# The beginning of a delta-rule attention and MoE kernel, put in one written list of steps: blocks turned by corner products, both first q loads early

## The chip, the cores and the metric

The kernel runs on one core of one Trainium2 chip. The metric is the time of one execution on the device, in microseconds (us). Engines: TensorE (PE: matmuls; PEld: its weight loads), VectorE (DVE), ScalarE (ACT), GpSimd (POOL) and SyncE (SP, which only issues DMAs). Each works through its own instructions in order and waits on semaphores for the others.

## The reference, cut to what matters

```python
# q, k, v: [4, 8, 768, 48] float32; beta: [4, 8, 768]; w_in [384, 2048], w_out [2048, 384]: float64
k_n = k / (norm(k) + 1e-6)
for t in range(768):                       # for each of 4 x 8 heads
    y[t] = q[t] @ state
    v_old = state.T @ k_n[t]
    state = state + beta[t] * outer(k_n[t], v[t] - v_old)
x = y, heads side by side                  # [3072, 384]
out = square(maximum(x @ w_in, 0)) @ w_out
```

## The kernel before, in words

**Units.** The 768 tokens are cut into 12 units of 64; a unit holds all 32 heads. Within a unit the recurrence is solved as a triangular system: the keys' products with one another, scaled by beta, form a unit lower triangle per head that is inverted.

A unit has these parts, each a Python generator that yields between steps:

- `load`, `load_q`, `load_v`, `load_beta` (lines 255 to 280) issue DMAs in pieces of 48 or 96 KB. k of units 0 and 1 comes over the queues of SP and ACT, all else over SP's (unit 0's beta over POOL's).
- `normalize` (line 282): squares on ACT, sums on DVE, square root on ACT, reciprocals and scaling on DVE.
- `static` (line 319): PE turns k and q (line 345), ACT copies them to `kq` (line 348), PE forms key by key and key by query products (line 361). In units 0 and 1 ACT copies both to `ap` (lines 397, 408), the key products go to DRAM and come back with one head and 32-token block per partition (lines 379, 386), and DVE masks the scores (line 411). Later units copy and mask in one DVE step (line 371).
- `invert_both` (line 430), units 0 and 1 together: DVE scales `lt` by beta (line 446), solves the 16 by 16 corners in 15 steps (lines 450, 452), scales (454) and turns the result (459). Then for each of the two units: another transposition (469), two bursts of 64 tiny matmuls (472, 479) with an ACT copy between (474), a subtraction (481), and DMAs of the inverse (492, 497). Of unit 0's four of line 497 ACT issues two and SP two.
- `invert` (line 500): the later units' solve, 31 pairs of DVE instructions (518, 519).
- `state_part` (line 776): `whole` (550 to 560 in unit 0, 564 to 586 later) completes the inverse, with products on the state in later units (608, 616), `solved` (632, 634) applies it to v, and `onward` forms keys times values for the state (649; 669 in unit 0, 654 later) and then y (660, 664). In unit 0 the keys' products stand ahead of y's on PE.
- `moe` (line 671): PE turns y (680), ACT and DVE split it in a high and a low part (683, 684); then 8 pairs of columns of w_in (line 714, 9 matmuls a step), ReLU, square and a split (721, 722, 724 on ACT, 693 on DVE) and, two pairs behind, w_out (line 701, 6 matmuls a step).

**Weights.** The float64 weights come as 28 pieces, 12 of w_in (512 columns) and 16 of w_out (384), and are made into a high and a low float32r part: `least` (ACT, 141), `words` (DVE, 149, 151, 153), `high` (ACT, 159), and `low` (PE and an ACT copy, 168). `low` has two forms: the long one adds three products on PE, the first of them of plain float32 (`ident` with tile `a`; 166, 167); the short one has two float32r products and needs `remainder` on DVE first (173). `words` writes tile `a` or `r`, of which there are two each, and from weight 14 on `a` alone (`room`, line 130). The first 8 weights take the long form; the other 20 go through `late`, with the short one.

**Order.** The schedule is manual: each engine gets its instructions in the order in which the program calls them. Up to unit 0's y it is written out (lines 797 to 870). From unit 1 on `weave` (line 757) merges the parts by a position between 0 and 1 for each step: the loop of unit 1 takes the MoE of unit 0, the remaining weights, `static` and part of the solve of unit 2, and the recurrence of unit 1; the loops of units 2 to 11 do the same without weights.

Of the kernel before, what the change touches and what calls it, by code (L numbers as in the profile page):

```python
# [8 lines left out]
F32 = mybir.dt.float32  # L9
# [8 lines left out]
SIGN = 2.0 ** 32  # L18


@with_exitstack
def kernel(
# [25 lines left out]
    P = 128  # L48
# [47 lines left out]

    ttile = []
# [20 lines left out]
    FIRST = 8  # L118
    LAG = 3
# [15 lines left out]
    def split_weights():  # L135
# [39 lines left out]
        def scaled(n):  # L175

            for _ in range(n):
                if done[0] < len(raws):
                    ready.append(least(done[0]))
                    done[0] += 1  # L180

        def worded(n):
            for _ in range(n):
                formed.append(words(*ready.pop(0)))

        def highs(n):
            for _ in range(n):
                waiting.append(high(*formed.pop(0)))

        def lows(n):  # L190
            for _ in range(n):
                low(*waiting.pop(0))

        def settled():
            highs(len(formed))
            lows(len(waiting))

        def early(n):

            for _ in range(n):  # L200
                scaled(2 - len(ready))
                worded(1)
                highs(1)
                lows(len(waiting) > LAG)

        def late():

            last = second = None
            while ready:
                now = words(*ready.pop(0))  # L210
                yield
                scaled(2 - len(ready))
                now = high(*now)
                if last:
                    remainder(*last)
                yield
                if second:
                    low(*second, formed=True)
                last, second = now, last
                yield  # L220
            remainder(*last)
            yield
            low(*second, formed=True)
            yield
            low(*last, formed=True)
            yield

        ready, formed, waiting, done = [], [], [], [0]
        return scaled, worded, highs, lows, early, settled, late()
# [31 lines left out]
    def load_q(d):  # L261

        d["qp"] = qp
        load_to(d["qp"], q, d, D)
# [54 lines left out]
    def static(d):  # L319

        u = d["u"]
        if u == 0:
            shared["blocks"] = dram.tile([4, 2, H2, HB, HB], F32, name="both", bufs=1)
        room = shared["blocks"][:, u] if u <= 1 else dram.tile([4, H2, HB, HB], F32, name="blocks")

# [11 lines left out]
        def transposed(parts, pair, into):  # L337
# [9 lines left out]
            for b in range(2):  # L347
                nc.scalar.copy(out=into[:, :, :, b], in_=pair[b])  # L348
# [26 lines left out]
        def to_blocks():  # L375
            rows = ap.rearrange("p c h x t -> p (c h) x t")
# [14 lines left out]
        if u <= 1:  # L391
            yield
# [9 lines left out]
            yield  # L402
# [7 lines left out]
            scores = ap.rearrange("p c h x t -> p (c h) x t")[:, :, 1]  # L410
# [522 lines left out]
```

## Time and profile before

| | before |
|---|---|
| runs, us | 627.93, 625.85, 626.23 |
| median, us | 626.23 |
| profiled execution: span, us | 627.0 |
| mean granted PE clock (1 is 2.4 GHz) | 0.963 |
| PE busy | 588.2 us (94%) |
| DVE busy | 419.1 us (67%) |
| ACT busy | 316.0 us (50%) |
| POOL busy | 29.4 us (5%) |
| DMA | 172464 packets, 49.32 MB |

The profiled execution is given by its span, from its first to its last instruction; the runs are others of the same kernel. Busy shares are means over the whole span: the clock's row on the page, in 40 slices, shows the lower level only in the first 8 and nothing but nines after them, and PE is at 9 of 10 from the ninth slice on, so the first 140 us are another stage than the rest. A row's time is from the start of the span; "idle before" names what ended an engine's wait.

### The profile page before, as it was taken

The page shows a single profiled execution, that of the slowest core. Times are in us where ns is not written, and L with a number is a line of the kernel's source. Part 1 is how long each engine was busy: PE and PEld are TensorE (multiplying, and loading weights), DVE is VectorE, ACT ScalarE, POOL GpSimd, SP SyncE. Part 2 cuts the span into 40 slices and gives each one's busy share as a digit, 9 for nine tenths or more (in the row PEclk, how much of TensorE's full clock was granted, in tenths as well). Part 3 has the DMA queues.
Part 4 walks back from the last instruction along what each step waited for, and adds up shares of the span by engine and source line. Part 5 has one row for each costly group of instructions (what it writes and reads, how often), then busy time and mean ns, then how long its engine had stood idle before and what let it go on. Part 6 is the DMA issues. An engine that isn't in the chain of part 4 may idle for free.

```text
span 627.0 us, 23868 instructions
## 1 busy us (share of the span) xinstructions
PE 588.2 (94%) x10392; PEld 556.1 (89%) x10392; DVE 419.1 (67%) x1131; ACT 316.0 (50%) x621; POOL 29.4 (5%) x52
## 2 busy tenths in 40 slices
PE   2948688999999999999999999999999999999997
PEld 2536587899999999999999999999999999999996
DVE  4795769785795795794885875876866956931211
ACT  4845577455345435536446445454545444355442
POOL 4000010001001001001001000010010010000000
PEclk9955789799999999999999999999999999999999
DMA  7797736114427217317227226226234143030101
GB/s 225 200 284 158 203 59 108 20 28 80 81 40 118 56 28 119 61 29 123 53 40 116 52 44 112 53 45 104 53 59 90 27 80 68 3 69 2 26 1 26
DMA packets 172464, 49.32 MB, mean 79 GB/s; under 512 B 164288, under 2 KB 167368, under 8 KB 172360
## 3 DMA queue, kind: packets, MB, share of 16 engines
q1 hardware_dynamic: 168840, 47.06, 37.5%
q8 instruction: 82, 1.34, 0.9%
q10 hardware_dynamic: 3392, 0.72, 0.6%
q14 instruction: 22, 0.18, 0.1%
q0 software_dynamic: 128, 0.01, 0.0%
HBM read 36.54 MB, written 10.49 MB: 75 GB/s over the span
## 4 chain that ended last, share of the span: by engine, by line
PE 87%; ACT 3%; DMA 3%; DVE 2%; issue 2%; SPq 1%; ACTq 0%; DVEq 0%
PE o L701 33%; PE h L714 32%; PE x L361 2%; PE x L608 2%; PE g L608 2%; PE x L632 2%; PE g L660 2%; PE g L361 1%; PE x L649 1%; PE x L582 1%; PE x L345 1%; PE h L571 1%; PE h L680 1%; PE g L345 1%; DMA qpad<-in_q_dram 1%
## 5 line engine op out<-in xcount | busy, mean ns | idle before, releaser
L701 PE MATMUL o<-w,h_h 128*128 128x384 f32 x768 | 203.8, 347 | 0.0
L714 PE MATMUL h<-x_h,w 128*128 128x256 f32 x1152 | 171.2, 285 | 0.0
L721 ACT ACTIVATE r<-h 128x512 f32<-128x512 f32 x96 | 57.5, 599 | 223.6 <-PE h L714 223.5
L693 DVE TENSOR_TENSOR h_l<-r,h_h 128x512 fp32r<-128x512 f32 x96 | 67.9, 707 | 148.1 <-ACT h_h L724 146.7
L714 PEld LDWEIGHTS h<-x_h,w 128*128 128x128 f32 x1152 | 156.4, 191 | 1.2
L701 PEld LDWEIGHTS o<-w,h_h 128*128 128x128 f32 x768 | 134.6, 189 | 3.2
L701 PE MATMUL o<-w,h_l 128*128 128x384 f32 x384 | 130.1, 339 | 0.0
L518 DVE SCALAR_TENSOR_TENSOR tmp<-lt,bt,z 128x126 f32<-128x126 f32 (+22 forms) x310 | 95.8, 309 | 7.8
L714 PE MATMUL h<-x_l,w 128*128 128x256 f32 x576 | 100.1, 283 | 0.0
L519 DVE TENSOR_TENSOR z<-z,tmp 128x126 f32<-128x126 f32 (+22 forms) x310 | 79.2, 255 | 10.6
L714 PEld LDWEIGHTS h<-x_l,w 128*128 128x128 f32 x576 | 82.3, 190 | 0.0
L701 PEld LDWEIGHTS o<-w,h_l 128*128 128x128 f32 x384 | 72.5, 189 | 0.0
L722 ACT ACTIVATE r<-r 128x512 f32<-128x512 f32 x96 | 60.7, 633 | 3.1
L724 ACT CAST h_h<-r 128x512 fp32r<-128x512 f32 x96 | 59.5, 620 | 3.0
L507 POOL MEMSET z<- 128x512 f32 x10 | 5.3, 532 | 447.6 <-DMA inv<-z 368.9
L654 DVE TENSOR_TENSOR state<-state,x 48x384 f32<-48x384 f32 x40 | 22.0, 551 | 0.9 <-PE x L649 0.3
L361 PE MATMUL x<-kq 48*64 48x64 f32 (+1 forms) x608 | 19.1, 251 | 1.2 <-ACT kq L348 0.7
L361 PEld LDWEIGHTS x<-kq 48*64 48x64 f32 x608 | 16.6, 147 | 3.4 <-ACT kq L348 1.1
L345 PE MATMUL x<-plus,kpad 64*128 64x64 f32 x96 | 6.7, 240 | 12.4 <-DVE kpad L309 11.3
L586 ACT ACTIVATE tt<-x 32x256 f32<-32x256 f32 x44 | 16.4, 374 | 1.4 <-PE x L582 0.8
L345 PEld LDWEIGHTS x<-plus,kpad 64*128 64x128 f32 x96 | 5.4, 152 | 13.0 <-issue 12.8
L141 ACT ACTIVATE w<-w 128x384 f32<-128x384 f32 (+1 forms) x28 | 16.6, 615 | 0.0
(143 smaller groups left out, 635.8 us busy)
## 6 DMA issues: line engine op xcount, KB each, us to landing
w<-in_moe_w_in_dram SPq DMA_DIRECT2D x12, 512.0 KB
w<-in_moe_w_out_dram SPq DMA_DIRECT2D x16, 384.0 KB
lt<-blocks SPq DMA_DIRECT2D x20, 256.0 KB
qpad<-in_q_dram SPq DMA_DIRECT2D x96, 48.0 KB
vt<-in_v_dram SPq DMA_DIRECT2D x48, 96.0 KB
out_dram<-a SPq DMA_DIRECT2D x46, 96.0 KB
kpad<-in_k_dram SPq DMA_DIRECT2D x88, 48.0 KB
blocks<-ap SPq DMA_DIRECT2D x40, 64.0 KB
```

The lines of the kernel that those rows point to most:

```text
L345: nc.tensor.transpose(pair[b][:, x, p], src[rows, c, 2 * p:2 * p + 2].rearrange("p a b -> p (a b)"), ident[rows, rows])
L361: nc.tensor.matmul(ps[j][to * C:(to + 1) * C, p, (x - first) * C:(x - first + m) * C], lhsT=kq[rows, c, p, b, 0], rhs=kq[rows, c, p, b, x: ...
L518: nc.vector.scalar_tensor_tensor(out=tmp, scalar=bt[:, s:s + 1], op0=ALU.mult, op1=ALU.mult, **factors)
L519: nc.vector.tensor_tensor(out=z[:, :nj, s + 1:], in0=z[:, :nj, s + 1:], in1=tmp, op=ALU.subtract)
L608: nc.tensor.matmul(dst[j][to, c, p], lhsT=d["kq"][rows, c, p, b, x], rhs=state[rows, b, c, p], start=(c == 0 and p == 0) if x else True, s ...
L654: nc.vector.tensor_tensor(out=state[rows, b], in0=state[rows, b], in1=ku[b][rows], op=ALU.add)
L693: nc.vector.tensor_tensor(out=h_l, in0=r, in1=h_h.bitcast(F32), op=ALU.subtract)
L701: nc.tensor.matmul(o[i], lhsT=a[:, e, i * P:(i + 1) * P], rhs=halves["wo", ft][w], start=(ft == 0 and n == 0), stop=(ft == FT - 1 and n == 2))
L714: nc.tensor.matmul(hp[:, e], lhsT=halves["wi", (kt, ft // EACH)][w][:, f], rhs=x[:, kt], start=(n == 0), stop=(n == 3 * KT - 1))
L721: nc.scalar.activation(out=r, in_=hp, func=AF.Relu)
L722: nc.scalar.activation(out=r, in_=r, func=AF.Square)
L724: nc.scalar.copy(out=h_h, in_=r)
```

## The change

The order of units 0 and 1 and of the weights becomes one list, `PLAN`, of 286 steps, each a letter that advances a part by one step: k, q, v, b with a digit are loads, f one weight's load; s, w, h, r, l are `least`, `words`, `high`, `remainder` and `low` of the next weight; A, B, n normalise units 0, 1, 2; a, b, x are their `static`; i is `invert_both`, j unit 2's `invert`, c and d the recurrences of units 0 and 1, m the MoE of unit 0, g unit 3's load and normalising. A `low` whose weight had its r takes the short form, any other the long one; there are three r.

Unit 0's and unit 1's key products no longer go through DRAM: PE multiplies picked columns of the identity with them so that both 16 by 16 corners of each block gather in one PSUM bank, and a DVE transposition writes `lt`. q of unit 1 is loaded into the third k tile, so that both q loads stand early on SP's queue; the first weights' loads stand between them. In unit 1, one of each two copies in `static` goes from ACT to DVE. In `invert_both`, unit 1's bursts are cut in halves, and all DMAs of the inverse are SP's. In unit 0, keys times values and the state's copies come a step behind y.

```diff
@@ -16,6 +16,15 @@
 
...
+PLAN = (
+    "k0 f k1 f A A A q0 f f b0 f A f B f b1 A q1 f A f f f a B B s B B f a s f B b a w s b v0 b a h b i f "
+    "i a i i i b i l i i s i i i i w i h i i i w l i w h i s s i f h c a r s c l s r w h f c f f l w k2 f "
+    "f f f s w q2 f b2 f f f f h c s l w h h s n w c s l n n n m h l o s f w s l l h m i n i w m l h m s "
+    "i w n m v1 h w i i l h r w m x i l w s m s g h x h x w w m l l s h s h s w m l b s m l m w l d h m s "
+    "m g s d h w m w l h l h g m j w m l h l s m j s g w m l h m j w l j j h m j g d j d j g l w m h s m "
+    "j d g s l j w h s m w j j w l j m h m h j d j m m j j j l j m j m j m j j j l j "
+)
 
@@ -94,6 +103,14 @@
...
+    picks = apool.tile([P, H, HB], F32, name="m", bufs=1)[:, :2]
+    nc.vector.memset(picks, 0.0)
+    for n in range(4):
+        for g in range(2):
+            rows = slice(n * HB, (n + 1) * HB)
+            nc.vector.tensor_copy(out=picks[rows, g, g * QB:(g + 1) * QB],
+                                  in_=eye[rows, n * HB + g * QB:n * HB + (g + 1) * QB])
+
@@ -172,61 +187,28 @@
...
+        ready, formed, waiting, done, summed = [], [], [], [0], set()
+
...
+        def rests():
+            part = next(y for y in waiting if y[0] not in summed)
+            remainder(*part)
+            summed.add(part[0])
+
+        def lows():
+            part = waiting.pop(0)
+            low(*part, formed=part[0] in summed)
+
+        return scaled, worded, highs, rests, lows
@@ -260,7 +242,7 @@
 
     def load_q(d):
 
-        d["qp"] = qp
+        d["qp"] = kpad[2] if d["u"] == 1 else qp
         load_to(d["qp"], q, d, D)
 
     def load_beta(d):
@@ -382,24 +361,26 @@
...
-            if u <= 1:
-                nc.sync.dma_start(out=lt, in_=shared["blocks"].rearrange("n u h s t -> (n u h) s t"))
-                return
...
         if u <= 1:
-            yield
-            transposed([(c, 0) for c in range(NC)], [x_tile(u) for _ in range(2)], kq[:, :, :, :, 0])
+            copy = [nc.scalar.copy, nc.vector.tensor_copy if u else nc.scalar.copy]
+            rows = ap.rearrange("p c h x t -> p (c h) x t")
+            transposed([(c, 0) for c in range(NC)], [x_tile(u) for _ in range(2)], kq[:, :, :, :, 0], copy)
             yield
             for c in range(NC):
                 for j, ps in enumerate(products(c, 0, 1)):
-                    nc.scalar.copy(out=heads(c, j)[:, :, 0], in_=ps)
-            to_blocks()
-            yield
-            if u == 1:
-                from_blocks(room)
-            yield
+                    copy[j](out=heads(c, j)[:, :, 0], in_=ps)
+            yield
+            if u == 0:
+                shared["corners"] = ps_g.tile([P, 2, PC], F32, name="g")[:, 0].rearrange("p (u h t) -> p u h t", u=2, h=H2)
+            for g in range(2):
+                for n in range(4):
+                    q = slice(n * HB, (n + 1) * HB)
+                    t = n % 2 * HB + g * QB
+                    nc.tensor.matmul(shared["corners"][q, u], lhsT=picks[q, g], rhs=rows[q, :, 0, t:t + QB],
+                                     start=(g == 0), stop=(g == 1), skip_group_check=True)
             yield
             transposed([(c, 1) for c in range(NC)], [x_tile(u) for _ in range(2)], kq[:, :, :, :, 1])
             yield
@@ -429,7 +410,7 @@
...
-        lt, bt = ds_[1]["lt"], ds_[0]["bt"].rearrange("p (g t) -> p g t", g=2)
+        lt, bt = apool.tile([P, HB, HB], F32, name="lt", bufs=1), ds_[0]["bt"].rearrange("p (g t) -> p g t", g=2)
@@ -441,8 +422,9 @@
...
-        zd, ld = corners(z), corners(lt)
+        zd, ld = corners(z), lt[:, :QB].rearrange("p t (g s) -> p g t s", g=2)
+        nc.vector.transpose(out=lt[:, :QB], in_=shared["corners"].rearrange("p u h t -> p t (u h)"))
@@ -465,19 +447,24 @@
...
+        yield
+
         for x in range(2):
             nc.vector.transpose(out=turned[x], in_=parts[x])
-            ps, places = quarters(2 * x)
-            for h, n, q in places:
-                nc.tensor.matmul(ps[q, h], lhsT=ds_[x]["ap"][q, h // H, h % H, 0, n % 2 * HB:(n % 2 + 1) * HB],
-                                 rhs=parts[x][q, h, QB:], start=True, stop=True)
-            nc.scalar.copy(out=mids[x], in_=ps)
-            yield
-            ps, places = quarters(2 * x)
-            for h, n, q in places:
-                low = slice(n * HB, n * HB + QB)
-                nc.tensor.matmul(ps[q, h], lhsT=turned[x][low, h], rhs=mids[x][low, h], start=True, stop=True)
-            yield
+            for way in range(2):
+                ps, places = quarters(2 * x)
+                for y, (h, n, q) in enumerate(places):
+                    if way:
+                        at = slice(n * HB, n * HB + QB)
+                        nc.tensor.matmul(ps[q, h], lhsT=turned[x][at, h], rhs=mids[x][at, h], start=True, stop=True)
+                    else:
+                        nc.tensor.matmul(ps[q, h], lhsT=ds_[x]["ap"][q, h // H, h % H, 0, n % 2 * HB:(n % 2 + 1) * HB],
+                                         rhs=parts[x][q, h, QB:], start=True, stop=True)
+                    if x and y == len(places) // 2 - 1:
+                        yield
+                if not way:
+                    nc.scalar.copy(out=mids[x], in_=ps)
+                yield
             nc.vector.tensor_tensor(out=parts[x][:, :, QB:], in0=parts[x][:, :, QB:], in1=ps, op=ALU.subtract)
             if x == 0:
                 ds_[0]["t1"] = mpool.tile([P, H2, HB], F32, name="h_h", bufs=3)
@@ -493,8 +480,7 @@
...
-                queue = nc.sync if x or n % 2 else nc.scalar
-                queue.dma_start(out=rows[q, :, n % 2 * HB:(n % 2 + 1) * HB], in_=parts[x][q])
+                nc.sync.dma_start(out=rows[q, :, n % 2 * HB:(n % 2 + 1) * HB], in_=parts[x][q])
@@ -648,10 +633,19 @@
                         nc.tensor.matmul(ku[b][j * C:j * C + n, c, p], lhsT=kp[rows, c, h, :n], rhs=uu[rows, c, h],
                                          start=True, stop=True)
+            if not u:
+                for b in range(2):
+                    nc.vector.tensor_copy(out=state[:, b], in_=ku[b])
+                return
             for b in range(2):
-                for j in range(2 if u else 0):
+                for j in range(2):
                     rows = slice(j * C, j * C + D)
                     nc.vector.tensor_tensor(out=state[rows, b], in0=state[rows, b], in1=ku[b][rows], op=ALU.add)
+
+        g = d["g"] if u else ps_g.tile([P, 2, PC], F32, name="g")
+        gy = areas([g[:, j] for j in range(2)], NP)
+        if 0 < u < units - 1:
+            keys_on_solved()
         for c in range(NC):
             for h in range(H):
                 p, j = h // 2, h % 2
@@ -665,8 +659,8 @@
                            in_=g[:, :, c * NP * D:(c + 1) * NP * D].rearrange("p j (n e) -> p j n e", n=NP))
             d["y"][c] = y
         if not u:
-            for b in range(2):
-                nc.vector.tensor_copy(out=state[:, b], in_=ku[b])
+            yield
+            keys_on_solved()
 
     def moe(d):
         x_h = mpool.tile([P, KT, 2 * P], F32R, name="x_h", bufs=1)
@@ -777,124 +771,69 @@
...
+    parts = dict(
+        s=scaled, w=worded, h=highs, r=rests, l=lows, f=lambda: fetch(1),
+        k0=lambda: new(0), k1=lambda: new(1), k2=lambda: new(2),
+        q0=lambda: load_q(ds_[0]), q1=lambda: load_q(ds_[1]), q2=lambda: load_q(ds_[2]),
+        b0=lambda: load_beta(ds_[0]), b1=lambda: load_beta(ds_[1]), b2=lambda: load_beta(ds_[2]),
+        v0=lambda: load_v(ds_[0]), v1=lambda: load_v(ds_[1]),
+        A=part("A", lambda: normalize(ds_[0])), B=part("B", lambda: normalize(ds_[1])),
+        n=part("n", lambda: normalize(ds_[2])), a=part("a", lambda: static(ds_[0])), b=part("b", lambda: static(ds_[1])),
+        x=part("x", lambda: static(ds_[2])), i=part("i", invert_both), j=part("j", lambda: invert(ds_[2])),
+        c=part("c", lambda: state_part(ds_[0])), d=part("d", lambda: state_part(ds_[1])),
+        m=part("m", lambda: moe(ds_[0])), g=part("g", lambda: loads(1)), o=late)
     with tc.manual_schedule(engines=engines):
+        for name in PLAN.split():
+            parts[name]()
+        before, inverse = begun["m"], begun["j"]
+        left = steps(NI + 1 - PLAN.split().count("j"), 0, I1 - 1) + [0.16]
+        for u in range(2, units):
...
```

Left out are the removed calls of lines 797 to 870, the removed helpers of the old order, and unchanged lines.

## Rows read from the trace of the kernel before

**Rows 1.** Windows: us, busy of PE, PEld, DVE, ACT, POOL, PE clock, DMA share, GB/s.

```profile
11.30:135.70 124.40, 101.28 (x2030) 85.60 (x2030) 96.46 (x232) 77.44 (x164) 2.73 (x4) 0.82 0.58 146
72.00:75.00 3.00, 2.25 (x23) 1.92 (x23) 2.83 (x6) 1.79 (x5) 0.00 (x0) 0.50 1.01 340
135.70:627.00 491.30, 486.85 (x8365) 470.49 (x8364) 319.31 (x890) 234.52 (x448) 18.88 (x27) 1.00 0.34 60
```

**Rows 2.** Source view of line 680, 120 to 150 us: durations ns, first and last start.

```profile
L680 PE MATMUL h<-plus,y x12: 221/222/273, 135.7 to 136.0; 64*128 64x64 f32 x12
```

**Rows 3.** Chain of waits, whole span: start us, length us, what.

```profile
150.33 2.12 PE o L701 x12
152.45 2.14 PE h L714 x18
156.33 1.08 PE x L608 x64
...
371.06 5.54 PE h L714 x45
...
416.20 5.54 PE h L714 x45
```

**Rows 4.** Chain of waits from 0 to 125 us, the same columns.

```profile
30.61 4.30 DMA qpad<-in_q_dram
...
45.43 3.46 issue
...
63.40 1.99 issue
...
76.31 1.73 PE x L479 x111
...
119.73 0.17 PE x L167
```

**Rows 5.** Timeline of SP, 0 to 130 us: start, length, issues.

```profile
0.80 5.49 SPq L253 DMA_DIRECT2D kpad<-in_k_dram  x8
6.79 1.41 SPq L127 DMA_DIRECT2D w<-in_moe_w_in_dram  x3
...
26.48 7.21 SPq L253 DMA_DIRECT2D qpad<-in_q_dram  x8
...
39.14 10.53 SPq L253 DMA_DIRECT2D qpad<-in_q_dram  x8
```

**Rows 6.** Timeline of DVE, 0 to 125 us: start, length, operation.

```profile
14.79 0.42 DVE L149 TENSOR_SCALAR a<-w 128x512 int32<-128x512 int32 x1
...
16.32 0.42 DVE L149 TENSOR_SCALAR r<-w 128x512 int32<-128x512 int32 x1
...
30.25 0.69 DVE L446 TENSOR_TENSOR lt<-lt,bt 128x512 f32<-128x512 f32 x1
...
39.71 0.69 DVE L454 TENSOR_TENSOR tt<-tt,bt 128x512 f32<-128x512 f32 x1
40.43 2.17 DVE L459 STREAM_TRANSPOSE lt<-tt 128x512 f32<-128x512 f32 x2
42.64 0.71 DVE L469 STREAM_TRANSPOSE h_h<-lt 128x512 f32<-128x512 f32 x1
```

**Rows 7.** Timeline of PE, 19 to 62 us, the same columns.

```profile
24.56 1.02 PE L166 MATMUL o<-a,plus 128*128 128x512 f32 x2
...
25.88 0.81 PE L166 MATMUL o<-r,plus 128*128 128x384 f32 x2
...
26.87 0.81 PE L166 MATMUL o<-a,plus 128*128 128x384 f32 x2
```

**Rows 8.** Timeline of ACT, 0 to 120 us, the same columns.

```profile
50.47 2.45 ACTq L497 DMA_DIRECT2D tt<-lt  x2
...
59.82 0.86 ACT L634 COPY vt<-h 128x384 f32<-128x384 f32 x2 [0.51 <-PE h L632]
```

**Rows 9.** Groups of instructions by line, DVE, 0 to 136 us.

```profile
L173 DVE TENSOR_TENSOR w<-a,w 128x384 fp32r<-128x384 f32 (+1 forms) x17 | 10.7, 631 | 0.4 <-ACT w L159 0.4
```

More of the change, by code (lines that the diff above doesn't have):

```diff
@@ L117 @@
     AHEAD = 14
-    FIRST = 8
-    LAG = 3
     def fetch(n):
@@ L173, in remainder, with scaled, worded, highs @@
             nc.vector.tensor_tensor(out=hl[:, 1], in0=a.bitcast(F32), in1=hl[:, 0].bitcast(F32), op=ALU.subtract)
[L175 to L210, printed above, removed]
-                yield
[L212 to L215, printed above, removed]
-                yield
-                if second:
-                    low(*second, formed=True)
-                last, second = now, last
-                yield
-            remainder(*last)
-            yield
-            low(*second, formed=True)
-            yield
[L225 to L229, printed above, removed]
+        ready, formed, waiting, done, summed = [], [], [], [0], set()
+        def scaled():
+            ready.append(least(done[0]))
+            done[0] += 1
+        def worded():
+            formed.append(words(*ready.pop(0)))
+        def highs():
+            waiting.append(high(*formed.pop(0)))
+        def rests():
[6 more added lines that the diff above has]
+        return scaled, worded, highs, rests, lows
     def split_bank():
@@ L335, in banks, with transposed @@
             return [g[:, 0], g[:, 1]]
-        def transposed(parts, pair, into):
+        def transposed(parts, pair, into, copy=(nc.scalar.copy, nc.scalar.copy)):
             pair = [x.rearrange("p (x n t) -> p x n t", x=2, n=NP) for x in pair]
@@ L347, in transposed @@
             for b in range(2):
-                nc.scalar.copy(out=into[:, :, :, b], in_=pair[b])
+                copy[b](out=into[:, :, :, b], in_=pair[b])
         def products(c, first, n):
@@ L375, in to_blocks @@
         def to_blocks():
+            room = dram.tile([4, H2, HB, HB], F32, name="blocks")
             rows = ap.rearrange("p c h x t -> p (c h) x t")
@@ L409, in static @@
             yield
-            scores = ap.rearrange("p c h x t -> p (c h) x t")[:, :, 1]
+            scores = rows[:, :, 1]
             nc.vector.tensor_tensor(out=scores, in0=scores, in1=mask[:, 1].unsqueeze(1).broadcast_to([P, H2, C]),
@@ L638, in onward, with keys_on_solved @@
         u, kp, ap, uu = (d[x] for x in ("u", "kp", "ap", "vt"))
-        g = d["g"] if u else ps_g.tile([P, 2, PC], F32, name="g")
-        gy = areas([g[:, j] for j in range(2)], NP)
-        if u < units - 1:
+        def keys_on_solved():
             ku = areas([x_tile(u) for _ in range(2)], NP)
@@ L779, in state_part @@
         yield
-        onward(d)
+        yield from onward(d)
         yield
@@ new lines, with part, step, new @@
+    scaled, worded, highs, rests, lows = split_weights()
+    begun = {}
+    def part(name, make):
+        def step():
+            if name not in begun:
+                begun[name] = make()
+            next(begun[name], None)
+        return step
+    def new(u):
+        ds_.append(load(u))
+    def late():
+        nonlocal split_early
+        split_early = False
+    parts = dict(
[9 more added lines that the diff above has]
+        m=part("m", lambda: moe(ds_[0])), g=part("g", lambda: loads(1)), o=late)
@@ L882 @@
[L882 to L884 removed]
+                woven.append((static(ds_[u + 1]), [-1, 0.155, 0.165]))
+                inverse = invert(ds_[u + 1])
+                woven.append((inverse, steps(n_i, I0, 1)))
                 left = steps(NI - n_i, 0, I1 - 1) + [0.16]
[L886 to L891 removed]
@@ L892 @@
-            parts += [(getting, L1 + steps(6, *N1) if u > 1 else [0.09] + steps(6, *N1)),
-                      (state_part(ds_[u]), [x / STEPS for x in (CHAIN if u > 1 else CHAIN1)])]
-            if before:
-                parts += [(before, [x / STEPS for x in range(OVER)] + [0.2, 0.21])]
-            parts.append((now, [x / STEPS for x in range(OVER, STEPS)] if u > 1 else steps(STEPS - OVER, 0, 1)))
-            weave(*parts)
+            woven += [(loads(u), L1 + steps(6, *N1)), (state_part(ds_[u]), [x / STEPS for x in CHAIN]),
+                      (before, [x / STEPS for x in range(OVER)] + [0.2, 0.21]),
+                      (now, [x / STEPS for x in range(OVER, STEPS)])]
@@ L898 @@
+            weave(*woven)
             before = now
```

108 lines of the change are left out of this document (5 added, 103 removed).

## The prediction

> **What bounds the kernel now.** I read the windows first [rows 1]. From 135.70 us on, where TensorE turns unit 1's result for its MoE (line 680, [rows 2]), PE is busy 486.85 of 491.30 us at full clock. That stretch, units 2 to 11, issues the same PE work after the change, so nothing is won there; the change counts by when PE reaches that point. Call it T. Before, T is 135.7. The new list puts one MoE step more ahead of it (half of the 2.12 in [rows 3], 1.06), so 136.8 is what the new T has to beat. From 11.3 to 135.7 PE is busy 101.28 of 124.40 us at a mean clock of 0.82: idle time and the lower clock level (0.50 from 72 to 75) are what can be won [rows 1].
>
> The chain of waits tells who is late [rows 4]: unit 0's q, bursts of tiny matmuls, and gaps that end with "issue" (3.46, 1.99), in which the profile shows no one that PE waits for.
>
> The sum is made against the profiled execution, whose span is 627.0. The runs are 625.85 to 627.93, their median 626.23, 0.8 below the span; I take 0.8 off at the end. About 0.3%, 1.9 us, is what a measurement here can tell from no change.
>
> **Blocks turned on chip, q early.** Removed are eight stores and one load through DRAM; the product with beta that waits for them starts at 30.25 [rows 6]. Added are 8 corner matmuls a unit and one DVE transpose out of PSUM. A long low of 512 columns takes 24.56 to 25.88, 1.32 [rows 7], of which the two float32r products are 0.46 (0.17 each at 384 columns, [rows 4]) and the fp32 one 0.86; a corner has 256 columns, so 0.43. Eight are 3.5 us one by one and 0.9 if the four quadrants run at once. I take 0.9: 32 matmuls of 48 columns on such tiles take 1.08 [rows 3], where that rate one by one asks 2.6. The transpose costs 0.7 (line 469) to 1.1 (line 459, strided); I take 1.1 [rows 6].
>
> But the list puts unit 1's q (b4) in front of the solve: PE must turn it, and DVE, which now does half of unit 1's copies, must copy it before its first solve instruction. SP's order: start 0.8, k 2.75, weight 0.47, k 2.75, weight 0.47, q 5.5, five weights 2.35, beta 2.8 (k's pace, 0.69 an issue), q 5.5 (k's pace) to 10.5 (behind nine weights) [rows 5]. Before, unit 0's q landed at 34.91, 1.2 after its last issue ended (33.69) [rows 4, 5]. So the new q lands between 24.6 and 29.6; I take 25.0, as five weights, with beta between, are ahead. Then its transposes (1.05), its copy (0.7, as line 469 for as many elements), the corners' transpose (1.1) and the product (0.7): the product ends at 28.6, against 30.94. **The DRAM trip gives way to a wait for q; 2.3 us are won.** The weights behind that q on SP come some 5 us later; DVE has no time for their words before. POOL's clearing of the solve's tile is long done, and no DMA moves to POOL.
>
> **The solve's tail.** From 30.94 to 39.71 the steps take 8.8 [rows 6]. The list adds one weight's words (14.79 to 16.32, 1.53, [rows 6]) and unit 1's second pair of score copies, for which DVE waits, an estimated 1.0: 39.9. Product and two transposes (0.7, 2.2): 42.8. Then another weight's words (1.53) and line 469 (0.7) [rows 6]: 45.0. What was won is spent on unit 1's scores and on words. The second burst takes 2.1 (1.73 for 111 of its 128 records, [rows 4]): 47.1, plus a gap.
>
> On the gap the rows come first: 3.46 inside this burst, 1.99 inside unit 0's y [rows 4]. I keep one of 2.0 here and drop the one in y. The burst ends at 49.1.
> The Trainium skill ("Runtime: NRT & Kernel Launch", Instruction fetch mechanics) says that code comes in 16 KiB blocks and that the cost of crossing into the next is mostly hidden. By that rule code loading would leave no gap here, and the time would be 622.0 instead of 624.0; no row shows the cause of the gaps.
>
> Before, from the gap's end and the burst's second half (1.06), 49.95, to the end of line 634, 60.68, the chain took 10.7 [rows 4, 8]. ACT spent 2.45 of it issuing two DMAs [rows 8], 0.6 of that with PE's products ready, and a low stood 0.5 in front of line 632. Both go: 9.6, so 58.7. The inverse's four DMAs, all on SP now, need 2.7 of issue and some 2 to land, hidden under lines 550 to 560; weights 16 on queue behind them, and their words are due past 80.
>
> From 58.7 PE has a full queue: y 1.1 and its latency 0.2, keys times values 1.1 (64 records as in [rows 3]; now behind y, so y is 1.1 earlier, and the state it feeds is read 30 us later), line 680 0.8, three narrow and two wide long lows at 1.0 and 1.3 [rows 7]: 8.8. **The first MoE matmul (line 714) starts at 67.5, against 72.0.**
>
> **The lows.** Before, 8 of 28 weights take the long low (three products, one fp32) and 20 the short one, after a DVE subtraction of 0.63 (line 173, [rows 9]). After, only 3 take the short one. The long costs 1.32 (512 wide) or 0.99 (384) [rows 7], the short, of two products at 0.17 (narrow, [rows 4]), 0.34, or 0.46 wide. Seventeen change over, 7 wide and 10 narrow: PE gets 7 x 0.86 + 10 x 0.65 = 12.5 us more, DVE at most 17 x 0.63 = 10.7 less.
>
> From the first MoE matmul to T, PE at full clock must do: 16 halves of line 714, 17.1 (2.14 per two), and 13 of line 701, 13.8 [rows 3]; 19 lows, 7 wide, 11 narrow and one short, 20.5; unit 1's two bursts, now in halves between MoE steps, 3.2 at most; unit 2's turning and unit 1's recurrence 10.3 (a full unit lasts 416.20 - 371.06 = 45.1, less 8 x 4.26 of MoE and 0.7 of line 680, [rows 3]). Sum 64.9. The same sum for before (12 steps, 14 short lows at 5.5, one burst) is 47.2, and it took 63.7: 16.5 were lost to gaps, half clock and waits. After, PE has 18 us more to run there, which fills waits and keeps the clock up; going through the list's order, each low's words and high part (1.5 and 0.5) are ready 0 to 2 us before PE comes to it. I take 2.2 lost (bounds 0 and 16.5). T = 67.5 + 64.9 + 2.2 = 134.6, 2.2 ahead of 136.8: 627.0 - 2.2 - 0.8 = **624.0**.
>
> The other edits cost nothing: the picks are filled while DVE waits for k; unit 1's k comes one weight later (0.5 of issue), and its squares' root stands behind unit 0's copies on ACT anyway.
>
> **The rivals.**
> Forecast, 624.0: 0.33.
> Gaps gone, 622.0: the burst has no gap, since SP waits for the inverse then and DMA should be quiet. For: the 3.46 fell among nine queued weights [rows 5]. Against: 1.99 came later, with few queued. 0.13.
> No change, 626.5: unit 1's q, behind five weights, lands at 27.5 instead of 25.0; the solve and all behind it are 2.5 us later, no earlier than by DRAM, so the turning on chip doesn't do what it says. For: the pace of 10.5 in [rows 5]. Against: fewer weights ahead. 0.28.
> Slower, 630.0: the long low reads tile a, of which there are two, so from weight 15 on DVE's words wait for PE's low two weights earlier; with the short one DVE freed it itself. Behind such a wait stand DVE's h_l, masks and solve steps of unit 2, and DVE has some 55 us of work in these 65 (18 weights' words 24, 25 solve steps 14, masks, normalising, recurrence and h_l 17). Thirteen such waits at 0.65 that come back to PE make 8.5 lost: T is 140.9, 4.1 behind. It decides from 4.4 lost on (136.8 - 132.4). For: DVE full, PE 12.5 heavier. Against: my walk finds each low ready. 0.26.
>
> **How the numbers follow.** Faster 0.33 + 0.13 = 0.46; same 0.28; slower 0.26. The range goes down to 618.0 (no gap and nothing lost, 619.8, and q or clock 1.8 earlier) and up to 632.0 (the slower case with q 2 us late). The forecast's own range is 622.0 to 626.0.
>
> **What would show it.** Right: the product with beta at about 28, held by DVE's copy of q and not by corners; line 714 first at 67 or 68; line 680's second group at 134 to 135, PE over 95% busy and at full clock between. Wrong: the product at 22 (q is no gate) or over 31; PE waiting for lines 149 to 159 between 80 and 130 (the rival with tile a); "issue" gaps of over 3 us in all; a stretch behind T that is not 490.2.

## The result and the profile after

The changed kernel takes 633.73 us in the median (632.07 to 635.47, 4 runs) against 626.04 for the kernel before (624.83 to 627.93, 4 runs): a ratio of 1.0121, interval 1.0078 to 1.0163. It is slower by 7.7 us. The profiled execution has a span of 633.3, against 627.0.

The windows of the changed kernel answer to [rows 1] (same columns). The second row is the stretch from the first MoE matmul (now line 708) to T, the third what is behind T:

```profile
11.30:139.20 127.90, 111.69 (x2102) 89.40 (x2102) 91.64 (x225) 76.98 (x162) 2.80 (x4) 0.88 0.55 137
70.10:139.20 69.10, 66.94 (x1131) 56.31 (x1129) 54.62 (x135) 46.80 (x95) 2.19 (x3) 1.00 0.46 98
139.20:633.30 494.10, 488.02 (x8359) 471.23 (x8358) 317.42 (x884) 235.44 (x449) 19.78 (x27) 1.00 0.33 59
```

The same stretch, first MoE matmul to T, in the kernel before:

```profile
72.00:135.70 63.70, 56.07 (x950) 51.18 (x949) 51.72 (x126) 39.53 (x80) 2.21 (x3) 0.87 0.38 71
```

T is the start of the transposes that answer to [rows 2], by the source view of line 674:

```profile
L674 PE MATMUL h<-plus,y x12: 221/223/272, 139.2 to 139.5; 64*128 64x64 f32 x12
```

So the first MoE matmul came 1.9 us sooner (70.1 for 72.0, where the prediction and this row begin; before, line 714 began at 71.81), and the way from there to T took 69.1 us for 63.7. Read the PE column: TensorE's busy time in that stretch grew from 56.07 to 66.94, and its idle time fell from 7.63 to 2.16. That is -1.9 + 10.9 - 5.5 = 3.5, T at 139.2. Behind T it is 494.1 against the 490.2 foreseen; e12 below shows that most of this belongs to the one execution (494.1 there became 491.2).

Why the start came only 1.9 us sooner is told by VectorE's timeline (start, length, operation, idle time before it and what ended it):

```profile
24.74 0.69 DVE L428 TENSOR_TENSOR lt<-lt,bt 128x512 f32<-128x512 f32 x1
...
36.33 2.10 DVE L441 STREAM_TRANSPOSE lt<-tt 128x512 f32<-128x512 f32 x2
...
40.10 0.70 DVE L453 STREAM_TRANSPOSE h_h<-lt 128x512 f32<-128x512 f32 x1
...
50.26 0.42 DVE L468 TENSOR_TENSOR lt<-lt,h 128x256 f32<-128x256 f32 x1 [7.55 <-PE h L459]
```

The product with beta starts at 24.74, 5.5 us before [rows 6], the two transposes at 36.33, 4.1 before, line 453 (469 before) at 40.10, 2.5 before. Then, behind one more weight's words, VectorE has nothing to do for 7.55 us: the subtraction waits for the second burst. It starts at 50.26; before, it started at 49.98. TensorE's first burst and VectorE's subtraction in the kernel before:

```profile
41.73 2.09 PE L472 MATMUL h<-lt,ap 32*32 32x16 f32 x128 [2.30 <-ACT w L141]
```

```profile
49.98 0.42 DVE L481 TENSOR_TENSOR lt<-lt,x 128x256 f32<-128x256 f32 x1 [1.13 <-PE x L479]
```

TensorE's timeline of the changed kernel says what TensorE did meanwhile:

```profile
37.34 2.07 PE L181 MATMUL o<-a,plus 128*128 128x512 f32 x2
38.42 1.42 PE L181 MATMUL o<-w,minus 128*128 128x512 f32 x1
39.63 0.63 PE L182 MATMUL o<-rest,plus 128*128 128x512 f32 x1
40.06 1.91 PE L181 MATMUL o<-r,plus 128*128 128x512 f32 x2
41.89 0.62 PE L181 MATMUL o<-w,minus 128*128 128x512 f32 x1
42.35 0.39 PE L182 MATMUL o<-h_l,plus 128*128 128x512 f32 x1
42.66 1.09 PE L461 MATMUL x<-lt,ap 32*32 32x16 f32 x109
45.89 0.50 PE L461 MATMUL x<-lt,ap 32*32 32x16 f32 x19 [2.14 <-issue]
46.86 1.68 PE L459 MATMUL h<-t,h_h 16*32 16x16 f32 x108 [0.46 <-ACT t L466]
49.72 0.51 PE L459 MATMUL h<-t,h_h 16*32 16x16 f32 x20 [1.18 <-issue]
```

From 37.34 to 42.66 TensorE does the low parts of two weights, at a mean granted clock of 0.55, in 2.7 and 2.6 us where [rows 7] have 1.32 for one. The first burst (line 461), whose operands VectorE had ready by 38.43, stands behind them in the same queue: it starts at 42.66, 0.9 later than before (41.73). Ahead of the low parts, in the same view of an earlier window, are unit 1's transposes of q, held by its load until 29.33, and both units' products with q, with a gap of 2.37:

```profile
29.33 0.34 PE L323 MATMUL h<-plus,kpad 64*128 64x64 f32 x1 [4.35 <-DMA kpad<-in_q_dram]
...
36.71 0.36 PE L339 MATMUL x<-kq 48*64 48x64 f32 x2 [2.37 <-issue]
```

SP's timeline shows where that q stands, behind five weights and beta:

```profile
15.13 0.60 SPq L142 DMA_DIRECT2D w<-in_moe_w_in_dram  x1
15.78 2.13 SPq L142 DMA_DIRECT2D w<-in_moe_w_out_dram  x4
17.95 2.79 SPq L256 DMA_DIRECT2D bt<-in_beta_dram  x4
20.79 7.48 SPq L235 DMA_DIRECT2D kpad<-in_q_dram  x8
```

### The profile page after: what moved, and what is told of

It is laid out like the page before. It is cut to its first block, busy times and chain, and to the rows that moved or that the text cites. A ratio compares the mean times of both kernels' runs of the same rounds, so it can differ in the third digit from the quotient of the medians.

```text
span 633.3 us, 23970 instructions
## 1 busy us (share of the span) xinstructions
PE 599.7 (95%) x10458; PEld 560.7 (89%) x10458; DVE 413.5 (65%) x1127; ACT 315.5 (50%) x618; POOL 30.4 (5%) x52
## 4 chain that ended last, share of the span: by engine, by line
PE 87%; DMA 4%; SPq 3%; ACT 2%; issue 2%; DVE 0%; ACTq 0%; DVEq 0%
PE o L695 33%; PE h L708 32%; PE x L618 2%; PE x L339 2%; SPq L235 2%; PE g L654 2%; PE g L594 2%; PE x L594 2%; PE o L181 1%; PE x L181 1%; PE g L339 1%; PE x L634 1%; DMA kpad<-in_k_dram 1%; DMA w<-in_moe_w_out_dram 1%; PE x L568 1%
## 5 line engine op out<-in xcount | busy, mean ns | idle before, releaser
L323 PE MATMUL x<-plus,kpad 64*128 64x64 f32 x104 | 8.1, 247 | 11.3 <-DVE kpad L291 11.3
L496 POOL TENSOR_SCALAR_AFFINE_SELECT z<-z 64x512 f32<-64x512 f32 x20 | 16.7, 833 | 1.3
```

## The experiments

All are edits of the written list unless told otherwise; a fragment of the list is shown. Ratios are to the kernel before, run on the same chip. Three theories were named. Theory 1: the long form of the low parts (12.5 us more on TensorE) sets T. Theory 2: VectorE and its two tiles a have no room for the subtractions. Theory 3: what stands in TensorE's queue in front of the first burst costs the early solve its gain.

**e1_short_lows**: the short form for weights 5 to 28.

```diff
-f h c s l w h h s n w c s l
+f h c s l w r h h s n w r r c s l
```

> The changed kernel (633.7) with r put ahead of the lows of weights 5 to 28, so that these all take the short form: 23 more subtractions on DVE (9 wide, 14 narrow, 13 us of work), 9 x 0.86 + 14 x 0.65 = 16.8 us less on PE. Theory 1, the long lows bound PE from unit 0's last steps (56 us) to T (139.2), where it is busy almost without a gap: T falls to 126 to 131, the time to 621 to 627. Theory 2, DVE and the two a tiles have no room for the subtractions: PE waits for DVE instead, T stays at 137 or later, the time at 632 to 636. Theory 3, unit 1's late q is what costs: the first MoE matmul stays at 69 to 70 and the time falls by no more than 2 us.

642.87 us, ratio 1.0273 [1.0229, 1.0316], T at 148.8. The waits (who waits for whom, us in all, times, longest), 45 to 150 us:

```profile
PE x L182 <- DVE w L189: 16.4, 13, 4.4
```

TensorE's work in the stretch fell to 61.29 us, and it lost 13.9 us in 75.2. Theory 1 alone falls; theory 2 has the cause, if not the size (632 to 636): the long forms are costly, the short ones cost more in this order, since TensorE then waits for a subtraction that stands in VectorE's queue behind other work.

**e2_q_first**: unit 1's beta and q right behind unit 0's q.

```diff
-q0 f f b0 f A f B f b1 A q1 f A f f f a
+q0 b0 b1 q1 f f f A f B f A f A f f f a
```

> The changed kernel with unit 1's beta and q issued right behind unit 0's q, ahead of five weights, and nothing else. Theory 3: PE's queue stood at the transposes of unit 1's q until 29.2 and everything behind them, the first burst included, with it; q lands at about 23, the burst that started at 42.7 starts at 38 to 39, and the time falls by 3 to 4 us to about 630. Theory 1: PE runs through its work from 56 us on anyway and most of the 4 us comes through to T as well, but no more than that, and the time stays above 629. If q were no gate at all: within 1 us of 633.7.

634.59 us, ratio 1.0137 [1.0104, 1.0170], T at 141.7. The chain of waits says why nothing came of it:

```profile
22.92 4.38 DMA w<-in_moe_w_in_dram
...
27.33 0.65 ACT w L156
27.98 0.54 ACT ap L374 x2
...
28.56 1.98 PE g L382 x16
...
30.56 0.73 DVE lt L427
...
31.31 0.70 DVE lt L428
```

The third weight now lands after the q's, ScalarE's scaling of it (line 156) waits, and the copies of unit 1's key products (line 374) stand behind that on ScalarE: the product with beta slips to 31.31. One queue's gate was exchanged for another's.

**e3_lows_behind**: the first two low parts behind both bursts.

```diff
-i a i i i b i l i i s i i i i w i h i i i w l i w h i s s i
+i a i i i b i i i s i i i i w i h i i i w i w h i l l s s i
```

> The changed kernel with the lows of the first two weights (l1, l2) moved behind the second burst of unit 0's inverse. They took 37.4 to 42.7 at the lower clock, in front of the first burst, whose data was ready at 37.4. Theory 3 (what stands in front of the burst on PE costs): the burst starts at 37.5 to 38, the first MoE matmul 2 to 4 us earlier, 630 to 632. Theory 1: the two lows cost the same PE time later, so T moves by less than 1.5 us.

629.91 us, ratio 1.0054 [1.0037, 1.0070]: about half of the loss is gone. The subtraction comes at 45.82, not 50.26, as theory 3 has it, and T at 136.9. But the first MoE matmul is at 69.6, only 0.5 sooner: the two low parts now stand between the second burst and the next products of unit 0, from 45.71 to 51.13, at a granted clock of 0.50. The other 1.8 us of T's 2.3 lie in the stretch behind, with 0.8 us idle and not 2.2, which theory 3 does not foresee. So e3 shows that the low parts hold up the burst; that this delay is what the time lost it does not show. e6 does.

**e4_all_three** (the edits of e1, e2 and e3 together):

> All three edits: short lows from weight 5 on, unit 1's q ahead of the weights, the first two lows behind the burst. If theories 1 and 3 both hold their gains add: 633.7 less 8 to 12 for the lows, less 3 to 5 for the start: 617 to 622, below the kernel before. If DVE has no room (theory 2): 629 or more.

648.26 us, ratio 1.0362 [1.0321, 1.0403], T at 155.5: the gain of e3 is lost under the other two.

**e5_corners_alone**: the kernel before with the corner products and the transpose from PSUM alone.

```diff
-            to_blocks()
...
-                from_blocks(room)
...
+                    nc.tensor.matmul(shared["corners"][q, u], lhsT=picks[q, g], rhs=rows[q, :, 0, t:t + QB],
+                                     start=(g == 0), stop=(g == 1), skip_group_check=True)
```

> The kernel before with one part of the change alone: corner products and one transpose from PSUM in place of the trip of the blocks through DRAM; order of the work, loads of q and keys times values as before. Theory 1 (the trip was hidden: VectorE had words of eight weights to make until 30.15 us and could not have begun the solve sooner in this order): the product with beta at 30.9 to 31.3 us (0.72 for the transpose is added), line 680's first transpose of unit 1's MoE between 135.2 and 136.5, time within 1.0 us of the kernel before. Theory 2 (the trip, or the eight DMAs it puts on SP in front of the weights and of q, was on the path): T at 133 or sooner, time 2 to 4 us less than before.

628.48 us, ratio 1.0024 [1.0001, 1.0047]. Theory 2 of this run falls: without the DRAM trip nothing is won, as VectorE has words to make until 32.5 us. Theory 1 has the cause, but not the size: the product is at 33.25 and not by 31.3, because VectorE waited 4.3 us for a low part (2.3 before), and the time is 1.3 over the kernel before, not within 1.0. The profiled execution was the slowest of its 11, with four gaps on TensorE in 40 to 80 us:

```profile
48.68 1.46 PE L489 MATMUL x<-t,h_h 16*32 16x16 f32 x92 [0.92 <-issue]
...
65.36 1.03 PE L670 MATMUL g<-vt,ap 64*64 64x48 f32 x56 [1.61 <-issue]
...
71.99 0.34 PE L367 MATMUL h<-kq 48*64 48x64 f32 x6 [2.03 <-issue]
...
76.27 0.30 PE L482 MATMUL x<-lt,ap 32*32 32x16 f32 x6 [2.13 <-issue]
```

**e6_queue_order**: on TensorE's queue, unit 0's products with q and the first low part go ahead of unit 1's transposes of q.

```diff
-h b i f i a i i i b i l i i s
+h a l b i f i i i i b i i i s
```

> The changed kernel, with two steps moved on TensorE's queue: unit 0's products with q and the low part of the first weight ahead of unit 1's transposes of q (which wait until 29 us for its load), so that TensorE does them while it would stand idle, and only unit 1's own products, and the second weight's low part, stand ahead of the first burst. Theory 3 (what stands on TensorE in front of the burst is what kept the earlier solve from coming through, and TensorE is full from there on): first burst at 37.3 to 38.5 us, the subtraction at 44 to 46, T at 131.5 to 134.5, time 5 to 8 us below the changed kernel (626 to 628.5), so below e3, since the 5.4 us of low parts come off TensorE's full stretch as well. Theory 2 (VectorE and the two tiles a pace the stretch from 50 to 139): the subtraction comes as early, but T stays at 136 to 137.5, time no better than e3 (629.5 to 631).

627.78 us, ratio 1.0021 [0.9993, 1.0049]: two fragments moved make the changed kernel equal to the kernel before. The first burst starts at 37.32, the subtraction is at 45.2, the first MoE matmul at 65.6 and T at 134.2: burst, subtraction, T and time are as theory 3 forecast them, and theory 2 (T at 136 to 137.5) falls. The windows from there to T and behind:

```profile
65.60:134.20 68.60, 66.88 (x1129) 56.31 (x1127) 54.50 (x136) 47.11 (x96) 2.49 (x3) 1.00 0.46 101
134.20:624.80 490.60, 486.17 (x8359) 469.66 (x8358) 317.29 (x884) 235.44 (x449) 18.93 (x27) 1.00 0.33 59
```

TensorE's work in the stretch is 66.88, as in the changed kernel (66.94), and 1.72 are idle. Of the 5.0 us by which T is sooner, 4.5 are won ahead of the stretch.

**e7_queue_and_q**: e6, with unit 1's q one weight behind unit 0's.

```diff
-q0 f f b0 f A f B f b1 A q1 f A f f f a
+q0 f b0 b1 q1 f f A f B f A f A f f f a
```

> As e6_queue_order, and unit 1's beta and q are loaded one weight behind unit 0's q, ahead of four weights (two weights more than in e2 land before the third weight is scaled). Theory 3: q lands at 24 to 26 us, all of unit 1's products are done by 33, but VectorE's own transposes (done 37.4 to 38.4) then gate the burst, so it gains 0 to 0.7 us over e6. If a weight is late instead (theory of e2: ScalarE's queue holds the key's copies behind the scaling of a weight that has not landed), the product with beta moves from 24.7 to 27 or later and the time is 2 to 4 us above e6.

627.52 us, ratio 1.0017 [0.9996, 1.0038]: the product with beta stays early (23.81; 24.24 in e6), and q sooner is worth nothing over e6 in time, though T is at 136.1 in the one profile, 1.9 later.

**e8_keys_first**: unit 0's keys times values ahead of y again.

```diff
-        if 0 < u < units - 1:
+        if u < units - 1:
             keys_on_solved()
```

> The changed kernel with another part undone: unit 0's keys times values stand ahead of y again. Theory 1 and 3 (TensorE is full from 50 us to T, so an exchange of two neighbours on its queue moves nothing): T within 0.5 us of 139.2, time within 1 us of the changed kernel. Rival (y ends the chain to the first MoE matmul): first matmul of line 708 0.8 to 1.3 us later (71.0 to 71.5), T and the time 0.8 to 1.5 us later.

633.15 us, ratio 1.0108 [1.0067, 1.0149]; first MoE matmul at 69.7, T at 139.0. This part of the change moves nothing.

**e9_one_ahead**: e6 with the splitting one weight further ahead; a weight's words also move into VectorE's wait for the second burst.

```diff
-b a w s b v0 b a h a l b
+b a w s b v0 b w a h h a l l b
```

> e6_queue_order with the weights' splitting one weight further ahead: the second weight's words in VectorE's gap between the key's copies and the transpose from PSUM, so that the low parts of weights 2 and 3 also lie ahead of the first burst, and the sixth weight's words in the gap in which VectorE waits for the second burst. Theory 1 (from the subtraction to T TensorE is full, so each long low part that it does before the burst comes off T): product with beta still at 24 to 24.8 us, subtraction at 44.5 to 46, T 1.5 to 2.8 us before e6's 134.2 (131.4 to 132.7), time 1.5 to 3 us below e6's. Rival (VectorE's own sum of work sets T, the words are only shifted): T within 0.7 us of e6's.

627.44 us, ratio 1.0019 [0.9993, 1.0045], T at 135.9: later than either theory had it. The expected gain is not there. The waits, 45 to 140 us, name what took its place:

```profile
PEld x L181 <- ACT w L174: 5.1, 3, 3.2
...
ACT kq L275 <- DMA kpad<-in_k_dram: 3.8, 1, 3.8
```

**e10_some_short**: e9 and five more short forms. **e11_k3_later**: e10, with unit 3's k behind unit 2's blocks on SP. Of e10 the fragment with weights 21 and 22:

```diff
-m g s d h w m w l h l h g m j w m l
+m g s d h w m w l h l h g m j r w r m l
```

> e9_one_ahead with the short form of the low part for five more weights (16, 17, 18, 21 and 22), those whose words stand where VectorE of e6 had idle time (84 to 88 and 97 to 105 us): 0.56 to 0.68 us more on VectorE each, 0.7 to 1.0 us less on TensorE each. Theory 1 and 2 together (short forms pay as long as VectorE has room where they stand, and cost where it has none, as in e1): T 2 to 4 us before e9's, time 2 to 4 us below e9's. Rival (e1's slope holds for each one: 23 short forms moved T by 9.6 us, so 0.4 us each): T 1.5 to 2.5 us behind e9's.

> e10_some_short with unit 3's load of k put behind the blocks of unit 2 on SP's queue (eight issues of 6.0 us stood ahead of them). Unit 2's blocks land some 6 us sooner, VectorE's idle time of 2.9 us ahead of the solve's first step goes, and the later steps run sooner. If VectorE bounds some of 105 to 134 us: T 0.5 to 2.5 us before e10's, time the same amount less. If TensorE alone sets T: T within 0.4 us of e10's.

633.91 us (1.0118 [1.0079, 1.0158]) and 636.7 us (1.0160 [1.0111, 1.0209]), T at 140.0 and 142.7: both are later than any of their theories had it. Both were badly placed, and show the mechanism of e1 in single rows. VectorE and then TensorE of e10:

```profile
106.73 0.25 DVE L505 SCALAR_TENSOR_TENSOR tmp<-lt,bt,z 128x31 f32<-128x31 f32 x1 [2.28 <-DMA lt<-blocks]
...
107.13 0.55 DVE L188 TENSOR_TENSOR w<-a,w 128x384 fp32r<-128x384 f32 x1
```

```profile
107.73 0.69 PE L181 MATMUL x<-w,plus 128*128 128x384 f32 x1 [3.73 <-DVE w L188]
...
110.05 0.80 PE L181 MATMUL x<-w,plus 128*128 128x512 f32 x1 [1.31 <-DVE w L188]
```

The remainder of weight 21 (line 188) stood on VectorE behind the solve's first step of unit 2, which waited for the blocks; TensorE stood 3.73 us behind it. In e11 it was ScalarE that stood in order before a k that had been moved back:

```profile
ACT y L276 <- DMA kpad<-in_k_dram: 8.7, 1, 8.7
```

**e12_changed_again**: the changed kernel, not edited.

> The changed kernel once more, nothing edited, for the 3.9 us behind T (issue gap at 166.3 us, half clock from 168.8 to 172.2). Theory A (they belong to that execution): the stretch behind T is 490.4 to 491.6 us, the span 629.5 to 631. Theory B (they belong to the kernel): again a gap of about 1 us and a fall of the clock in 160 to 175 us, stretch 493 to 494.5 us.

632.32 us, ratio 1.0095 [1.0063, 1.0127], span 632.0. Its windows, first MoE matmul to T and behind T:

```profile
71.30:140.80 69.50, 66.97 (x1131) 56.21 (x1129) 54.66 (x136) 47.08 (x96) 2.44 (x3) 1.00 0.46 97
140.80:632.00 491.20, 486.41 (x8359) 469.69 (x8358) 316.61 (x884) 235.30 (x449) 19.09 (x27) 1.00 0.33 59
```

Theory A for the stretch behind T: 491.2, as in e8 (139.0 to 630.2). The 494.1 of the first profile was that execution's, with one gap of 1.04 and a granted clock of 0.55 for 3.4 us behind it; in the profiles of the edited lists the stretch is 490.0 to 493.2. The span was 1 us over the 629.5 to 631 expected, because T here is 140.8. One kernel thus had T at 139.2 and at 140.8 in two executions: differences of T below 1.6 us between single profiles show nothing.

**e13_k2_early**, **e14_two_short**, **e15_blocks_first**: e9 with unit 2's k ahead of the first inverse's stores; then two of e10's short forms put ahead of that solve step; then the blocks ahead of unit 3's k.

```diff
-h i s s w i f h c a r s c l s r h f c f f l w k2 f
+h i s s w k2 i f h c a r s c l s r h f c f f l w f
...
-h g m j w m l
+h g m r r j w m l
```

> e9_one_ahead with unit 2's load of k moved on SP's queue ahead of the stores of the first inverse, which hold that queue until the subtraction at 45.7 us while nothing is moved. In e9 k landed at 64.0 us, and ScalarE, in order, waited 3.8 us for it in front of the cast of a weight, and TensorE 2.4 us for that cast. Queue theory (in this stretch the cost is what stands in order in front of the next piece of TensorE's work): k lands by 50 us, those waits go, the first MoE matmul of line 708 comes at 65.0 to 66.2 (e9 67.7), T at 133 to 134.5 (e9 135.9), time 1.2 to 2.8 us below e9. Rival (sum theory: TensorE's work between 45 and T is what counts, and another wait takes the place): first MoE matmul moves, T within 0.7 us of e9's.

> e13_k2_early with two of e10's five short forms, weights 21 and 22, their remainders placed ahead of the solve's first step of unit 2 on VectorE and not behind it (in e10 they stood behind that step, which waited until 106.7 us for the blocks, and TensorE waited 3.7 and 1.3 us for them). Queue theory: a short form pays where its remainder is not held up: T 1.0 to 2.0 us before e13's. Rival (short forms cost on VectorE whatever their place, 0.4 us each by e1): T 0.5 to 1.5 us behind e13's.

> e14_two_short with unit 3's load of k behind unit 2's blocks on SP, as in e11, and k's squares (which stood on ScalarE so early in e11 that it waited 8.7 us for that k) put behind as well. Queue theory: the blocks land at 97 to 100 us and not at 105, the solve's first steps stand in VectorE's idle time, ScalarE does not wait for k; T 0.3 to 1.5 us before e14's. Rival: T not better than e14's, as TensorE has no waits left there that the blocks end.

625.66 us (0.9988 [0.9960, 1.0015]), 625.71 (0.9994 [0.9968, 1.0019]) and 626.53 (1.0004 [0.9977, 1.0030]). e13's T is 134.2, as the queue theory had it, and the waits of e9 are gone, though its first MoE matmul moved by only 0.5 (67.2, forecast 65.0 to 66.2). In e14's profile the first MoE matmul is at 65.4 and T at 132.1, 2.1 us before e13's:

```profile
65.40:132.10 66.70, 64.08 (x1121) 54.91 (x1119) 52.41 (x131) 45.37 (x92) 1.96 (x3) 1.00 0.42 90
132.10:623.20 491.10, 486.64 (x8359) 470.12 (x8358) 317.41 (x886) 234.84 (x448) 19.25 (x27) 1.00 0.34 59
```

But 1.8 of that stands already in front of the first MoE matmul, where e14 differs from e13 in nothing, and the medians are the same: a gain of the two short forms is not shown. e15 gains nothing over e14 (T 133.9); the solve's first step is at 104.89 there and at 103.82 in e14. All three are level with the kernel before; none is shown to beat it.

## Why the prediction was wrong

**What bounds the kernel**: right. The stretch behind T is 491.2 in two profiles of three (e8 and e12), 1.0 over 490.2, and all the rest happens ahead of T.

**Blocks on chip, q early**: the failing step is "PE must turn it, and DVE, which now does half of unit 1's copies, must copy it before its first solve instruction". The halved copies are not "one of each two" of unit 1, but those of its keys and key products alone; q's and its scores' stay on ScalarE, so the 1.0 for "unit 1's second pair of score copies" was not there either. The product started at 24.74 and ended at 25.4, not 28.6. That q landed late (29.3, not 25.0) did not touch VectorE. It touched TensorE.

**The solve's tail**: the sum followed VectorE alone, to 45.0 for the end of line 469 (453 now). VectorE had done it at 40.80. The term that is missing is TensorE's queue in front of the first burst: unit 1's q, both units' products with a gap, and two long low parts at half clock, until 42.66, 4.2 behind VectorE's transposes. The burst then had a gap of its own, 2.14, and the second one 1.18, where one of 2.0 had been taken. So the second burst ended at 50.2 where 49.1 was forecast: two errors, 4.2 us early and 5.3 us late, that nearly cancelled by luck. e3 and e6 show it from the other side: with that queue rearranged the subtraction comes at 45.8 and 45.2, 4.4 and 5.0 us sooner, and in e6, where nothing of it was put behind the burst, so does the first MoE matmul (65.6 for 70.1).

**The chain to the first MoE matmul**: forecast 58.7 for the end of unit 0's copy, 59.97 measured; 8.8 of queue behind it, 10.2 measured, the clock being at its lower level until 62.9 (0.51 from 50.3 on). The 1.3 of the first, in which the 1.1 of the burst is contained, and the 1.4 of the second are the 2.6 by which the first MoE matmul missed 67.5.

**The lows**: the loss of 2.2, a choice between 0 and 16.5, came out at 2.16 (2.53 in e12), which is in part luck. The rival with tile a fell as it was priced: VectorE waited four times, 2.6 us in all, for a tile a that TensorE had still to read, and 0.5 us of TensorE's waits end with the words behind. The work, forecast at 64.9, is 66.9 in four profiles of this order of work (66.94, 66.97, 66.92 in e8, 66.88 in e6): mis-sized by 2.0. Counted in the changed kernel from each matmul's start to the next one's, idle time left out, the 16 halves of line 708 have 18.1 (forecast 17.1), the 13 of line 695 14.2 (13.8), the lows 21.6 (20.5), the two bursts 2.7 (3.2) and the rest 10.4 (10.3): the 2.0 are in the first three.

So T = 134.6 + 2.6 + 2.0 = 139.2. The first miss is the larger. The old list spent the time in which VectorE waited for DRAM on words, and had 14 low parts done when the first MoE matmul began; the new one has nine and carries five more, in the long form, into a stretch that TensorE fills. That price was in the sum. The prize that was to pay for it, a start 4.5 us sooner, came to 1.9, or 0.7 in e12; in e6 it came to 6.4, and the time is then level with the kernel before. e5 adds that the DRAM trip, taken away by itself, was worth nothing: VectorE's words covered it.

**From T to the time**: the sum set the profiled execution of the kernel before, span 627.0, against a median time of 626.23, "0.8 below the span". This is a second step that failed. A time is 1.7 to 1.9 us longer than its span in every run that lists both (635.07 and 633.3 in the changed kernel's profiled one), so that an execution with this span has a time of about 628.7, 2.5 above the median; the runs of the kernel before that list it have median spans of 624.8 to 625.5. T before was read from an execution some 2 us longer than most. With T at 134.6 and 490.2 behind it the span is 624.8 and the time about 626.6, level with the kernel before, and not 624.0. e6 and e13 show just this: T at 134.2 in both, spans of 624.8 and 625.7, and medians of 627.78 and 625.66 beside 627.21 and 626.94 for the kernel before.

The rival "no change" had q late, as it was, but through VectorE. "Gaps gone" fell with its reason: in 34 to 50 us the profile has 2.37, 2.14 and 1.18, and while the last two lasted the DMA engines moved 0 GB/s.

## What to carry to other kernels

Cost a step that is made sooner on every in-order queue that its result has to pass, not only on the engine that gains: here VectorE was done 4 us sooner and TensorE's queue, which held the next load's products and two slow pieces of filler, kept it from being used. Here filler put ahead of a piece that waits for a load filled the wait (e6); between that piece and the burst it held up the chain (37.34 to 42.66). A shorter form that needs a second engine is longer where its piece on that engine stands behind something that waits (3.73 us for one in e10); that it gains when it stands in front is not shown (e14).

## What was not expected of the hardware

TensorE's gaps in bursts of tiny matmuls move with the order. Unit 0's first burst of 128 pauses in every profile of the new list, for 0.87 us (e6) to 2.55 (e2), but for e7's, where its 128 go through in 1.90; in the kernel before and in e5 it does not pause. The second burst pauses in every profile, for 0.91 to 3.46 us.

The page of the changed kernel has a DMA queue of "instruction" packets (packets, MB, share):

```profile
q8 instruction: 82, 1.34, 0.9%
```

These are 82 packets of 16 KiB, and TensorE's 10458 matmuls and 10458 weight loads make 255 for each; by that mean a burst of 128 with its loads takes one packet. The packets of the changed kernel's trace end at 35.46, 44.32 and 48.15, and the gaps of 2.37, 2.14 and 1.18 end at 36.71, 45.89 and 49.72. So it is throughout: of the 50 "issue" gaps of 0.5 us and more that TensorE has between 11 and 141 us in all 17 profiles, 45 end 1.25 to 1.94 us after the end of such a packet. That ties these gaps to the loading of code, whether DMA is busy (405 GB/s in the first) or not (0 in the other two); no run moved the code by itself, and what delays a packet stays open. The Trainium skill ("Runtime: NRT & Kernel Launch", Instruction fetch mechanics) has the cost of crossing a block of code as mostly hidden. The trace agrees for most: of the 16 packets up to 141 us three are followed by such a gap. In e7 the packet ended at 35.1, while the burst still waited for VectorE until 36.66, and the gap is not there.

The clock stood at its lower level, a mean of 0.52 in 45 to 55 us of e6, behind those pauses. From the first MoE matmul to T its mean was 1.00 where TensorE was idle for 2.2 us (changed kernel) or 1.7 (e6), 0.91 where it was idle for 13.9 (e1); in e10, with TensorE busy 5.96 of 10 us in 105 to 115, it fell to 0.66 again.
